# Pooled attention with a routed feed-forward: the row index moved from GpSimd to VectorE, the row fetch put one step later, and one set of transposes put behind the last values pass

## The chip, the core and the metric

The kernel runs on one core of a Trainium2 chip. The metric is the device time of one execution in microseconds (us); lower is better. Engine names below are those of the profile: PE is TensorE's matmul, PEld its weight load, DVE is VectorE, ACT is ScalarE, POOL is GpSimd, SP is SyncE, which issues most of the DMAs.

## What is computed

The reference has two blocks, one behind the other, in float32. Cut to what matters:

```python
# q, k, v: (8, 8, 1152, 64)
q_pool = q.reshape(B, H, S // 2, 2, D).mean(axis=3)
scores = np.matmul(q_pool, k.transpose(0, 1, 3, 2)) / np.sqrt(D)
scores = scores - np.max(scores, axis=-1, keepdims=True)
attn = np.exp(scores)
attn = attn / (np.sum(attn, axis=-1, keepdims=True) + 1e-09)
x = np.matmul(attn, v).transpose(0, 2, 1, 3).reshape(8, 576, 512)

# w_gate: (512,), w1: (512, 1024), w2: (1024, 512), capacity: 128
scores = np.einsum('bsd,d->bs', x, w_gate)
out = x.copy()
for b in range(B):
    top_idx = np.argpartition(-scores[b], capacity)[:capacity]
    xe = x[b, top_idx]
    h = np.maximum(xe @ w1, 0.0)
    ye = h @ w2
    g = 1.0 / (1.0 + np.exp(-scores[b, top_idx]))
    out[b, top_idx] = x[b, top_idx] + g[:, None] * ye
```

So each of the eight batches has an attention over pairs of pooled queries, then a score for each of its 576 rows; the 128 rows with the highest scores go through a two-layer feed-forward, scaled by a gate, and are added to themselves.

## The kernel before

**Halves.** The attention works on pairs of heads, four pairs for a batch, 32 pairs in all. A pair is done in two halves of 288 queries (`s` 0 and 1), so there are 64 halves, and the loop of `run` (L1322) goes over them with one more turn at the end. In each turn PE first computes the scores of half `h` (L818: 36 matmuls, 72 instructions) and then the values of half `h - 1` (L836, the same number). ACT takes the exponent of the scores in nine pieces (`p`, L825) and copies the result of the values pass out of PSUM (`two`, L844). All PSUM results go through four buffers handed out in turn by `banks`, so a matmul may have to wait until ACT has read an earlier buffer. POOL adds up parts of `p` (`acc`, L857, three instructions a half), adds the two planes of `two` (`av`, L846), multiplies with the gate's weights (`prod`, L925), normalizes (`x`, L956, in halves with `s` 1) and pools the next queries (`qp`, L732, in halves with `s` 0). DVE folds `p` and `acc` into sums (L862 twice, L872), transposes (`avb` L915, `kT` L735, `qT` L739), and computes `rec` (L954), `red`, `part` and `total` (L979, L981, L893). ACT spreads `total` into `sums` (L902) in halves with `s` 1, and copies `sum` into `groups` (L887) in halves with `s` 0.

**Units.** When the four pairs of a batch are done, `gated` starts `routed` for it, a Python generator that emits the second block in steps ("units"). Each `yield` ends a step; `units` advances every waiting generator by one step, the newest batch first. In each turn `units` is called twice: `units(mid=True)` between the scores and the values, and `units(mid=False)` at the end of the turn. A step that ended in "mid" or "hidden" goes on in the first of these, the others in the second. The order in which instructions are emitted is the order on each engine; nothing is reordered afterwards (`manual_schedule`).

For a batch below the last two, the steps are, one after the other:

- `line` (L1007, DVE) and `groups` of it (L887, ACT), then `total`, a row of scores written to DRAM and read back to all partitions (`sc_row`, `gate_sc`, SP's DMAs at L1032 to L1035);
- the gate's bound (L1069, POOL) and the comparisons that give each row its rank (`cmp` L1083 and L1092, `tie` L1102, DVE), for blocks 0 and 1 of rows, then 2 and 3 one half later, then 4 another half later, with the gate's exponent on ACT (L1115) and its sum on POOL (L1118);
- ranks and gates to DRAM and back to all partitions (`lines`, L1131 and L1135);
- one half later, the search (L1166, two instructions on DVE, the first yields the row's number, the second its gate), the index of that row in the whole output (L1175, POOL) and the fetch of the 128 rows (L1183, a DMA with an index, issued by POOL);
- a step with nothing in it, then in the middle of a turn the transposes of the fetched rows (L1197, four matmuls) and their copy `xeT` (L1200, ACT); in the middle of the next turn the first layer (L1208, 64 instructions) with its `hT` (L1216, ACT); in the middle of the next turn the second layer (L1221, 16 instructions) with `y` (L1240, ACT);
- at the end of that turn the sum (L1245, POOL) and the scatter of the rows (L1246, a DMA with an index, issued by POOL).

The batches are counted from 0. Batch 5 (`B - 3`) stops before its second layer, which is kept for the end (`waiting`), where the last batches leave PE without attention work. Batch 6 (`B - 2`) has fewer steps between, and batch 7 uses matmuls for its row of scores and its search (L1054, L1152). After the loop, `run` emits what is left of batches 5, 6 and 7 in an order written out by hand (L1397 to L1409).

The turn behind the last half (`h == n_halves`) starts with what is left of the pair before, calls `units` twice (L1362, L1363), and then emits the last values pass (`weighted`), its transposition (`drained`) and the rest.

Of the kernel before, what the change touches and what calls it, by code (L numbers as in the profile page):

```python
# [27 lines left out]
def _any_scores(  # L28
# [451 lines left out]
    in_pair = [(j, t) for j in range(2) for t in range(NF)] + [(0, NF)]  # L480
    upcoming = load_pair(*pairs[0])
    run(prepare_pair(upcoming))
    preparing = iter(())
    routing = iter(())
# [23 lines left out]
    for n, (b, hp) in enumerate(pairs):  # L508
        pair = upcoming
        run(preparing)  # L510
        if hp == 0:
            x = xpool.tile([P, NT, Dm], F32, name="x")
        for i, (j, t) in enumerate(in_pair):
            now = {"pair": pair, "j": j, "t": t, "x": x}
            advance(now)
            if two is not None and two["t"] == NF and two["pair"]["hp"] == NPAIR - 1:
                run(routing)
                routing = routed(two["pair"]["b"], two["x"])
            one, two = now, one
            if i == 0 and n + 1 < len(pairs):  # L520
                upcoming = load_pair(*pairs[n + 1])
                preparing = prepare_pair(upcoming)
            if n == 0 and i == 0:
                load_weights()
            if i >= 3:
                next(preparing, None)
            next(routing, None)
    for _ in range(2):
        advance(None)
        one, two = None, one  # L530
    run(routing)
    run(routed(B - 1, x))


class _Plain:
# [461 lines left out]
    def routed(self, b, part):  # L997


        nc, ffn, Sp, NT, NF = self.nc, self.ffn, self.Sp, self.NT, self.NF  # L1000
        tiles = [(t, P if t < NF else self.TAIL) for t in range(NT)]
        mid = "mid" if b < self.B - 2 else True
# [134 lines left out]
        for s0, w in self.slots:  # L1137
# [3 lines left out]
            if b == self.B - 1:  # L1141

                nc.vector.tensor_tensor(
                    out=pick[:, :, 0:w],
                    in0=self.slot_f[:, s0 : s0 + w].unsqueeze(1).broadcast_to([P, NT, w]),
                    in1=rank[:, :].unsqueeze(2).broadcast_to([P, NT, w]),
                    op=ALU.is_equal,
                )
                yield True
                ps = self.banks()[:, 0, 0:2]  # L1150
                for t, rows in tiles:
                    nc.tensor.matmul(  # L1152
                        ps[0:w, :],
                        lhsT=pick[0:rows, t, 0:w],
                        rhs=meta[0:rows, t, :],
                        start=(t == 0),
                        stop=(t == NT - 1),
                    )
                nc.scalar.copy(index[0:w, :], ps[0:w, 0:1])
                nc.scalar.copy(own_gate[0:w, :], ps[0:w, 1:2])  # L1160
            else:
                yield True

                found = self.small.tile([P, 1], F32, name="found_token")
                for of, to in ((self.token_line, found), (lines[:, :, 1, :], own_gate)):
                    nc.vector.scalar_tensor_tensor(  # L1166
                        out=pick.rearrange("p t i -> p (t i)").rearrange("p (i t) -> p i t", t=NT)[0:w],
                        in0=lines[0:w, :, 0, :],
                        scalar=self.token[0:w, s0 // P : s0 // P + 1],
                        in1=of[0:w, :, :],  # L1170
                        op0=ALU.is_equal,
                        op1=ALU.mult,
                        accum_out=to[0:w, :],
                    )
                nc.gpsimd.tensor_scalar(  # L1175
                    out=index[0:w, :],
                    in0=found[0:w, :],
                    scalar1=float(b * Sp),
                    scalar2=None,
                    op0=ALU.add,  # L1180
                )
            xe = ffn.tile([P, self.Dm], F32, name="xe")
            nc.gpsimd.indirect_dma_start(  # L1183
                out=xe[0:w, :],
# [122 lines left out]
    def run(self):  # L1307
        nc = self.nc
# [13 lines left out]
        for h in range(n_halves + 1):  # L1322
            if h < n_halves:
                n, s = divmod(h, 2)
                if s == 0:
                    pair = upcoming
                    if pair["hp"] == 0:
                        part = self.ffn.tile([P, self.NPAIR, self.QB], F32, name="part")
                    pair["part"] = part
                else:  # L1330
                    loaded = None
                    if n + 2 < len(pairs):
                        loaded = self.load_pair(*pairs[n + 2])
                        self.load_values(loaded)
                    if n > 1:
                        self.stored(halves[h - 4]["pair"])
                if h > 1:
                    next(weights, None)
                half = {"pair": pair, "s": s}
                halves.append(half)  # L1340
                self.scores(half)
                if h > 1:

                    of = halves[h - 2 - s]["pair"]
                    if s == 0:
                        of["groups"] = self.side_by_side(of["sum"].rearrange("p j n -> p (j n)"))
                    else:
                        self.spread(of)
                self.units(mid=True)
                if h > 2:  # L1350
                    self.gated(halves[h - 3])
                self.folded(half)
                if h > 1:
                    self.multiplied(halves[h - 2])
                if s == 0 and loaded:
                    upcoming = loaded
                    self.prepare_pair(upcoming)
            else:
                self.stored(halves[h - 3]["pair"])
                self.gated(halves[h - 3])  # L1360
                self.multiplied(halves[h - 2])
                self.units(mid=True)  # L1362
                self.units(mid=False)  # L1363
            if h > 0:
                done = halves[h - 1]
                self.weighted(done)
                self.drained(done)
            if h == n_halves:
                self.multiplied(done)
                self.gated(halves[h - 2])  # L1370
            if 1 < h < n_halves and s == 0:
                done["pair"]["total"] = self.added(done["pair"]["groups"])
            if h == n_halves:
                self.normalized(done["pair"])
            elif h > 2 and s == 1:
                self.normalized(halves[h - 2]["pair"])
            if h < n_halves:
                self.units(mid=False)
# [93 lines left out]
```

## Time and profile before

| What | Value |
|---|---|
| Median of three runs | 707.29 us (706.78 to 708.1) |
| Time of the profiled execution | 706.64 us |
| Span of the profiled execution | 704.8 us |
| Granted TensorE clock in it | 0.998 |
| PE busy | 694.4 us, 99% of the span |
| POOL busy | 485.1 us, 69% |
| DVE busy | 496.5 us, 70% |
| ACT busy | 444.5 us, 63% |
| Index (L1175), 7 instructions | 6.4 us on POOL, mean 920 ns; POOL idle before them 20.2 us |
| Fetch (L1183), 8 instructions | 9.1 us on POOL; 3.4 to 5.8 us from the instruction's start to landing, median 4.8 us |
| Scatter (L1246), 8 instructions | 8.3 us on POOL |

How to read it: the span is what the profiler saw between the first and the last instruction; the execution's own time is 1.84 us longer. A busy share says how much of the span an engine was at work, not that its work set the end. A line of the timeline has a start and a duration in us, the engine, the line of the kernel, the operation, the tiles (written<-read), the shape, a count, and in brackets the engine's idle time just before and what ended it. A line of the chain of waits has a start, a duration and what ran. Idle time of an engine other than PE costs nothing by itself here, unless PE comes to wait for it.

### The profile page before, as it was taken

The numbers are of one execution on the slowest core, as the hardware profiler recorded it, in microseconds if no ns is written. First come the engines' busy times: TensorE is split into PE (matmuls) and PEld (weight loads), VectorE is DVE, ScalarE is ACT, GpSimd is POOL, SyncE is SP. The second block draws the span as 40 slices with busy tenths as digits, with TensorE's granted clock in tenths as the row PEclk, the third lists the DMA queues.
The fourth block names the chain that finished last, engine by engine and source line by source line (L and its number), as shares of the span: only waits on it lengthen the run. The fifth ranks groups of instructions, "written<-read, shape, count | busy, mean of one in ns | idle before, by whom it ended". The sixth has DMA issues, their size and how long they took to land.

```text
span 704.8 us, 23397 instructions
## 1 busy us (share of the span) xinstructions
PE 694.4 (99%) x9948; PEld 516.8 (73%) x9948; DVE 496.5 (70%) x793; ACT 444.5 (63%) x963; POOL 485.1 (69%) x452
## 2 busy tenths in 40 slices
PE   8999999999999999999999999999999999999996
PEld 5668899996758866688656887578775787766573
DVE  3877777996559965498754988559774697689540
ACT  6677778777547775477746776467754777477210
POOL 5877777868658695586955779467874877686520
PEclk9999999999999999999999999999999999999999
DMA  8888887858486483756928468382775728432200
GB/s 175 172 178 180 171 166 137 146 116 161 85 149 111 85 162 75 145 97 111 172 40 159 81 129 160 66 148 61 161 130 85 135 56 169 83 72 62 45 31 35
DMA packets 389490, 82.86 MB, mean 118 GB/s; under 512 B 376640, under 2 KB 376640, under 8 KB 389376
## 3 DMA queue, kind: packets, MB, share of 16 engines
q1 hardware_dynamic: 387872, 76.49, 58.1%
q0 software_dynamic: 1280, 4.20, 1.8%
q8 instruction: 80, 1.31, 0.8%
q10 hardware_dynamic: 224, 0.59, 0.3%
q14 instruction: 34, 0.28, 0.1%
HBM read 69.65 MB, written 11.59 MB: 115 GB/s over the span
## 4 chain that ended last, share of the span: by engine, by line
PE 89%; POOL 5%; issue 2%; DMA 1%; ACT 1%; DVE 1%; SPq 0%; POOLq 0%; DVEq 0%; ACTq 0%
PE ps L836 36%; PE ps L818 36%; PE ps L1208 8%; PE ps L1221 7%; POOL acc L857 2%; ACT p L825 1%; DMA kb<-in_k_dram 1%; DMA xe<-out_dram,index 1%; PE ps L1197 1%; POOL prod L925 1%; POOL x L956 0%; POOL av L846 0%; DVE fold L862 0%; POOL index L1175 0%; SPq L759 0%
## 5 line engine op out<-in xcount | busy, mean ns | idle before, releaser
L825 ACT ACTIVATE p<-ps 128x576 f32<-128x576 f32 x576 | 320.2, 695 | 1.7 <-PE ps L818 1.3
L818 PE MATMUL ps<-qT,kT 64*64 64x288 f32 x4608 | 295.2, 404 | 0.2 <-ACT p L825 0.2
L836 PE MATMUL ps<-p,v_sb 64*64 64x288 f32 x4608 | 294.6, 403 | 0.0
L857 POOL TENSOR_TENSOR acc<-p 128x576 f32<-128x576 f32 x192 | 266.3, 1417 | 15.4 <-ACT p L825 15.1
L836 PEld LDWEIGHTS ps<-p,v_sb 64*64 64x64 f32 x4608 | 215.5, 133 | 65.3 <-ACT p L825 9.2
L818 PEld LDWEIGHTS ps<-qT,kT 64*64 64x64 f32 x4608 | 208.0, 132 | 73.0 <-ACT p L825 15.4
L862 DVE TRANSPOSE_TENSOR_REDUCE fold<-p 128x54 f32<-128x1728 f32 x64 | 126.0, 1969 | 50.2 <-ACT p L825 50.2
L862 DVE TRANSPOSE_TENSOR_REDUCE fold<-acc 128x54 f32<-128x1728 f32 x64 | 125.3, 1957 | 46.0 <-POOL acc L857 45.8
L844 ACT COPY two<-ps 128x576 f32<-128x576 f32 x64 | 40.9, 639 | 156.9 <-PE ps L836 143.8
L846 POOL TENSOR_TENSOR av<-two 128x288 f32<-128x288 f32 x64 | 51.2, 800 | 96.5 <-ACT two L844 94.9
L915 DVE STREAM_TRANSPOSE avb<-av 128x288 f32<-128x288 f32 x64 | 29.4, 460 | 66.5 <-POOL av L846 66.5
L956 POOL TENSOR_TENSOR x<-avb,rec 128x576 f32<-128x576 f32 x32 | 37.1, 1159 | 40.3 <-DVE rec L954 27.9
L1208 PEld LDWEIGHTS ps<-xeT,w 128*128 128x128 f32 x512 | 57.8, 192 | 2.7 <-ACT p L825 2.6
L1208 PE MATMUL ps<-xeT,w 128*128 128x128 f32 x512 | 59.3, 277 | 0.0
L1221 PE MATMUL ps<-w,hT 128*128 128x512 f32 x128 | 57.3, 598 | 0.0
L925 POOL TENSOR_TENSOR prod<-avb,w_gate 128x288 f32<-128x288 f32 x64 | 51.5, 805 | 0.6 <-DVE avb L915 0.6
L902 ACT ACTIVATE sums<-total,tiny 32x18 f32<-32x18 f32 x124 | 38.1, 308 | 15.9 <-DVE total L893 14.2
L732 POOL TENSOR_TENSOR qp<-qb 128x576 f32<-128x576 f32 x31 | 43.8, 1414 | 2.2 <-DMA qb<-in_q_dram 2.2
L1221 PEld LDWEIGHTS ps<-w,hT 128*128 128x128 f32 x128 | 23.6, 190 | 28.1 <-issue 25.8
L735 DVE STREAM_TRANSPOSE kT<-kb 128x1152 f32<-128x1152 f32 x31 | 42.5, 1370 | 0.0
L887 ACT COPY groups<-sum 32x36 f32<-32x36 f32 x124 | 27.1, 219 | 6.7 <-DVE sum L872 5.2
L981 DVE TENSOR_TENSOR part<-red,rec 128x18 f32<-128x18 f32 x32 | 27.0, 845 | 1.1
(95 smaller groups left out, 290.6 us busy)
## 6 DMA issues: line engine op xcount, KB each, us to landing
kb<-in_k_dram SPq DMA_DIRECT2D x124, 144.0 KB
qb<-in_q_dram SPq DMA_DIRECT2D x124, 144.0 KB
v_sb<-in_v_dram SPq DMA_DIRECT2D x124, 144.0 KB
out_dram<-x SPq DMA_DIRECT2D x128, 72.0 KB
lines<-row_rank SPq DMA_DIRECT2D x7, 640.0 KB
w<-in_moe_w_dram SPq DMA_DIRECT2D x8, 512.0 KB
sc_row<-row SPq DMA_DIRECT2D x7, 288.0 KB
acc<-in_q_dram ACTq DMA_DIRECT2D x2, 288.0 KB
```

The costliest lines, as they stand in the source:

```text
L732: nc.gpsimd.tensor_tensor(out=qp[:, :, :], in0=pair["q"][:, :, 0, :], in1=pair["q"][:, :, 1, :], op=ALU.add)
L735: nc.vector.transpose(kT.rearrange("p (c g i) -> p c g i", c=self.NC, i=BLK), pair["k"].rearrange("p (g c) d -> p c g d", c=self.NC),)
L818: nc.tensor.matmul(sc[keys, j, 0:n], lhsT=pair["kT"][rows, c * P + keys.start : c * P + keys.stop], rhs=pair["qT"][rows, qs], start=True, ...
L825: nc.scalar.activation(p[:, c // G, c % G, :, :], sc[:, :, 0:n], AF.Exp, scale=self.scale)
L836: nc.tensor.matmul(av[j * self.D : (j + 1) * self.D, e, 0:n], lhsT=half["pair"]["v"][keys, j, c, :], rhs=half["p"][keys, c // G, c % G, j, :],
L844: nc.scalar.copy(two[:, :, :], av[:, :, 0:n])
L846: nc.gpsimd.tensor_tensor(out=half["av"][:, :], in0=two[:, 0, :], in1=two[:, 1, :], op=ALU.add)
L857: nc.gpsimd.tensor_tensor(out=acc[:, u, :], in0=units[:, 0, u, :], in1=units[:, 1, u, :], op=ALU.add)
L862: nc.vector.tensor_reduce(fold[:, a, :], of.rearrange("p u (m d) -> p (u m) d", d=BLK), AX.X, ALU.add, apply_transpose=True,)
L925: self.nc.gpsimd.tensor_tensor(out=pair["prod"][:, ns, :], in0=pair["avb"][:, ns, :], in1=self.w_gate[:, hp : hp + 1, :].broadcast_to([P, ...
L1208: nc.tensor.matmul(pv[:, f, 0:w], lhsT=self.w1[:, c, (f0 + f) * P : (f0 + f + 1) * P], rhs=xeT[:, c, 0:w], start=(c == 0), stop=(c == self ...
L1221: nc.tensor.matmul(ps[0:w, 0 : self.Dm], lhsT=hT[:, f, 0:w], rhs=self.w2[:, f, :], start=(f == 0), stop=(f == self.NFC - 1),)
```

## The change

The index is computed by VectorE instead of GpSimd. For batches 0 to 5 a `yield True` follows it, so the fetch and everything after it is emitted one turn later than before. In the turn behind the last half, the two calls of `units` go behind the last values pass.

```diff
@@ -1172,13 +1172,16 @@
                         op1=ALU.mult,
                         accum_out=to[0:w, :],
                     )
-                nc.gpsimd.tensor_scalar(
+                nc.vector.tensor_scalar(
                     out=index[0:w, :],
                     in0=found[0:w, :],
                     scalar1=float(b * Sp),
                     scalar2=None,
                     op0=ALU.add,
                 )
+                if b < self.B - 2:
+
+                    yield True
             xe = ffn.tile([P, self.Dm], F32, name="xe")
             nc.gpsimd.indirect_dma_start(
                 out=xe[0:w, :],
@@ -1359,13 +1362,13 @@
                 self.stored(halves[h - 3]["pair"])
                 self.gated(halves[h - 3])
                 self.multiplied(halves[h - 2])
-                self.units(mid=True)
-                self.units(mid=False)
             if h > 0:
                 done = halves[h - 1]
                 self.weighted(done)
                 self.drained(done)
             if h == n_halves:
+                self.units(mid=True)
+                self.units(mid=False)
                 self.multiplied(done)
                 self.gated(halves[h - 2])
             if 1 < h < n_halves and s == 0:
```

In the order of instructions on each engine this gives the following. Lines of the kernel before are used.

- POOL, batches 0 to 5: L1175 is gone. L1183 moves from behind `av` of a half with `s` 0 to behind `x` of the next half, which has `s` 1. For batches 0 to 4, L1245 and L1246 move from behind `av` of a half with `s` 0 to behind `x` and L1069 (the next batch's) of the next half. Batch 6: L1175 is gone, L1183 stays.
- PE, batches 0 to 5: L1197 and L1208 each stand one turn later, and so does L1221 for batches 0 to 4. Batch 6: L1197 stands behind the last values pass instead of ahead of it.
- ACT, batches 0 to 5: `xeT` moves from behind `groups` of a half with `s` 0 to behind `sums` (and, for batches 0 to 4, behind the next batch's `groups` of `line`) of the next half; it stands ahead of `two` as before. `hT` and, for batches 0 to 4, `y` move by one turn too. Batch 6: `xeT` moves behind the last `two`.
- DVE: seven instructions of 128x1 more, each behind the two of the search.
- SP: its list of DMAs stays the same.

## The prediction

> **What bounds the kernel now.** I read the page's busy shares first, then the chain of waits, then the timeline of each engine around one fetch (batch 1) and around the end. PE is busy 99% of the span, so the change can only remove or add the few places where PE stands still. In the chain, a pass of 72 instructions takes 4.37 us when nothing disturbs it. Batch 4's transposes show a typical disturbance:
>
> ```profile
> PE 694.4 (99%) x9948; PEld 516.8 (73%) x9948; DVE 496.5 (70%) x793; ACT 444.5 (63%) x963; POOL 485.1 (69%) x452
> ...
> 500.73 4.38 PE ps L836 x72
> 505.11 4.61 PE ps L818 x71
> 509.72 0.59 PE ps L1197 x4
> ```
>
> The pass ahead of L1197 is 0.24 us too long. For batches 0, 1, 2 the same reading gives 0.10, 0.17 and 0.25 us. Batch 3: from L836 at 397.11 (4.39 us) five more passes should end at 423.35, and L1197 starts at 424.04: 0.69 us. Batch 5: 590.75 + 4.37 = 595.12 against 595.73: 0.61 us. Together 2.06 us. Why they wait is seen in batch 1:
>
> ```profile
> 245.51 0.92 POOL L1175 TENSOR_SCALAR index<-found_token 128x1 int32<-128x1 f32 x1 [2.96 <-DVE pick L1166]
> 246.71 1.14 POOL L1183 DMA_INDIRECT xe<-out_dram,index  x1 [0.28 <-POOL index L1175]
> 247.88 4.15 POOL L857 TENSOR_TENSOR acc<-p 128x576 f32<-128x576 f32 x3
> 239.09 0.64 ACT L844 COPY two<-ps 128x576 f32<-128x576 f32 x1 [2.48 <-PE ps L836]
> 248.16 0.64 ACT L844 COPY two<-ps 128x576 f32<-128x576 f32 x1 [2.22 <-PE ps L836]
> ```
>
> POOL stands 2.96 us for the search, and fetches late. The last L836 matmul before the two `two` lines starts at 238.59 and 247.34: `two` follows after 0.49 us normally, after 0.82 us where the fetch runs. In batches 0, 1, 2, 4, 5 it is 0.25 to 0.43 us late in this way; PE's loss is some 0.15 us less than the lateness (0.39 late, 0.25 lost in batch 2). In batches 3 and 5 the fetch itself lands too late.
>
> At the end PE waits twice more:
>
> ```profile
> 653.20 0.63 PE L1197 MATMUL ps<-ident,xe 128*128 128x128 f32 x4 [0.61 <-DMA xe<-out_dram,index]
> 664.28 1.21 PE L1054 MATMUL ps<-diag,ones 128*128 128x288 f32 x4 [0.35 <-DVE rank_parts L1076]
> ```
>
> **Part 1, the index on DVE.** POOL loses 7 x 0.92 us and the wait in front of it. DVE gets 7 instructions; the nearest row, a DVE TENSOR_SCALAR of one element (L1283), took 0.14 us, so 1 us in all. Of this only 0.15 us for each of batches 1 to 4 lies in a chain that matters (below). The index now stands behind both searches (the second takes 0.89 us), so the fetch could start at once only where POOL is free: for batch 6 it starts 0.1 us earlier.
>
> **Part 2, the fetch one turn later.** I walk through batch 1 with its own rows. POOL needn't wait for the search, so `acc` starts when `av` is done, some 3.5 us earlier. The fetch then stands behind `x`. Its start comes out at 254.65, with PE wanting the rows at 260.6: 5.9 us, against landings of 3.4 to 5.8 us. It ends at 255.8, before the next `two` is due at 256.55. So I take all 2.06 us as saved (bounds 0 and 2.06).
>
> A fetch under other DVE work is what a rule of the Trainium skill warns of (SBUF — State Buffer, "Who interferes with whom"): while VectorE runs an instruction that takes the port pair shared with GpSimd, GpSimd cannot write a DMA's descriptors. The eight fetches here took 1.06 to 1.27 us, two-microsecond folds beside them, so the rows show none of it; by the rule a fetch beside a copy of 1.37 us (L735's time) would be that much later and the sum up to 1.4 us a batch higher.
>
> **Part 3, what moves with it.** This is where I expect the loss. The sum L1245 and scatter L1246 come one turn later too, from a half in which POOL has been idle for 7 us to one where `acc` waits behind them:
>
> ```profile
> 205.60 1.28 POOL L1245 TENSOR_TENSOR xe<-y,xe 128x512 f32<-128x512 f32 x1
> 207.16 1.05 POOL L1246 DMA_INDIRECT out_dram<-xe,index  x1 [0.28 <-POOL xe L1245]
> ...
> 216.62 0.24 POOL L1069 TENSOR_SCALAR gate<-gate_sc 128x5 f32<-128x5 f32 x1
> 216.83 4.21 POOL L857 TENSOR_TENSOR acc<-p 128x576 f32<-128x576 f32 x3
> 219.62 1.97 DVE L862 TRANSPOSE_TENSOR_REDUCE fold<-p 128x54 f32<-128x1728 f32 x1
> 221.51 1.93 DVE L862 TRANSPOSE_TENSOR_REDUCE fold<-acc 128x54 f32<-128x1728 f32 x1
> ```
>
> L1069 ends some 0.45 us earlier than before (216.4, the half's fold is done sooner). Then 1.25 + 0.28 + 1.04 us: `acc` starts at 219.0 instead of 216.83 and ends at 223.2. DVE's fold of `acc`, which followed its other fold without a gap at 221.51, now waits to 223.23: 1.72 us later. From there to 239 DVE has only two gaps, 0.27 and 0.85 us, both behind POOL work (gate, `acc`) that itself follows DVE's `rec`. So the 1.72 us stays in the chain (bounds 0, if the gaps and POOL's shorter queue take it in, and 2.2). The search starts at 246.28 instead of 244.56 and ends, index included, at 248.15. The folds follow at 248.55 and 250.45 (before 252.06, having waited for POOL), `x` at 253.4 (255.02), the fetch to 255.8, `acc` at 255.83 (256.14), its fold at 260.03 (260.33), and so `total` at 264.6 (264.91). The time won on POOL is used up.
>
> Now the cover that is gone. ACT's queue in that half:
>
> ```profile
> 265.30 1.27 ACT L902 ACTIVATE sums<-total,tiny 32x18 f32<-32x18 f32 x4 [2.24 <-DVE total L893]
> 266.60 0.85 ACT L887 COPY groups<-line 32x18 f32<-32x18 f32 x4
> ...
> 273.76 0.64 ACT L844 COPY two<-ps 128x576 f32<-128x576 f32 x1 [4.01 <-PE ps L836]
> ...
> 257.22 4.54 PE L818 MATMUL ps<-qT,kT 64*64 64x288 f32 x72
> 261.70 7.41 PE L1208 MATMUL ps<-xeT,w 128*128 128x128 f32 x64
> ```
>
> `sums` waits for `total`, and `two` is behind it. This was free, since the first layer's 7.34 us of matmuls made the half long: `two` was due at 273.76. With L1208 one turn later the half holds only the transposes: scores from 256.22 to 260.59, transposes to 261.18, values (4.53 us behind them, as in the chain of before) to 265.71, `two` due 0.35 us later at 266.05. ACT's queue: `sums` 265.0 to 266.3, `groups` to 267.1, `xeT`, now here too (0.57 us), to 267.65. So `two` is 1.6 us late, the next exponents are as late, and the next scores pass finds no free buffer. By the relation above PE loses 1.6 - 0.15 = 1.45 us.
>
> Batches 1 to 4: 4 x 1.45 = 5.8 us. Batch 5 has no `groups` of `line` there (-0.85) and PE has L1021 more (0.33): 0.42 late, 0.3 lost. Batch 0 has no scatter ahead: its folds run 1.7 us earlier, `xeT` ends at 265.95 in these times, just before 266.05: 0. Sum 6.1 us. Bounds: 0, if `total` comes as early as for batch 0 in all, and 6.1 + 5 x 0.6 = 9.1, if DVE's chain is another 0.6 us later (the tie at 398.58 took 1.57 us where others took 0.62).
>
> A rule speaks for more loss: the same page and section say that a VectorE instruction with two SBUF inputs and a GpSimd instruction that reads SBUF block each other wholly. The row: `tie`, which now meets L1245, took 0.34 us alone and 0.62 to 0.92 us beside POOL's work, so it is lengthened already and I add nothing; by the rule up to 1.28 us a batch would be added to the chain.
>
> **Part 4, the end.** Before, from the values pass at 648.00 to L1054 at 664.28: 16.28 us. Now two values passes without a break (2 x 4.37), transposes 0.59, L938 0.24, L1221 5.40: 14.97. PE could be at L1054 1.31 us sooner. L1054 needs `diag`, the end of a chain over POOL and DVE that ran almost without a gap from 619 on; with batch 5's L1208 now inside the turn after, DVE has its first comparisons done before that turn ends and is some 2 us ahead there, 1.4 us ahead at batch 6's fetch. So I take 1.2 us of 1.31. Without that lead only batch 6's 0.1 us is left: bounds 0.1 and 1.31.
>
> **Sum.** -2.06 - 1.2 + 6.1 = +2.84 us. Profiled: 706.64 becomes 709.5 (span 704.8 to 707.6). The median of the runs is 0.65 us above the profiled execution: 707.29 + 2.84 = 710.1 us.
>
> **Rivals.** *A, the lead reaches PE* (faster): POOL's 3.5 us and the gaps take in the scatter, every batch goes like batch 0, nothing is lost: 707.29 - 3.26 = 704.0. For it: POOL is idle 20.2 us at the index. Against: DVE's rows without gaps. Chance 0.16. *B, a wash*: `two` comes only 0.8 us late, 4 x 0.65 = 2.6 us lost, batch 5 nothing: 707.29 - 3.26 + 2.6 = 706.6. For it: the lateness is a difference of long sums; if POOL reaches L1245 a microsecond sooner it halves. Chance 0.17. *C, worse*: the delayed `sums` of the search's own half also passes its `two`: it ends at 247.65 where `two` is due at 247.83, a margin of 0.18 us. From 0.33 us (margin plus 0.15) more delay PE pays there too; with 1 us more in batches 1 to 4, 4 x 0.67 there and as much behind it: 715.5. Chance 0.10; its near part is in the range. *D, it doesn't do what it says*: the fetch, elsewhere now, holds up `two` again, and the 2.06 us isn't saved: 712.2. Against: 0.75 us between its end and `two`. Counted in the forecast's own spread.
>
> **How the numbers follow.** Forecast 0.57 (708.7 to 713), A 0.16, B 0.17, C 0.10. A measurement of this kernel can tell 0.2%, 1.4 us, from no change, so "same" is 705.9 to 708.7. Faster 0.17 (A and a little of B), same 0.16, slower 0.67. The range is 706.0 to 713.0: below lies A, above most of C; its own bounds would be 707 to 713.
>
> **What would show it.** In the changed profile: no index on POOL and no wait there; the fetch some 5.9 us before its transposes and `two` back at 0.49 us; `acc` behind the scatter near 2 us late; then, in the half of the transposes, `sums`, `groups` and `xeT` right up to a late `two`, and a scores pass of some 5.8 us instead of 4.37 behind it, for batches 1 to 4 and not batch 0. If these passes are 4.37 us, A holds.

## The result and the profile after

The changed kernel takes 726.0 us (median of 6 runs, 725.32 to 728.61), beside 706.76 us for the kernel before (6 runs, 705.41 to 708.1): ratio 1.028, 95% interval 1.0258 to 1.0303. The prediction said slower, by 2.8 us; it is slower by 19.2 us. The profiled execution has a span of 726.0 us, 21.2 us more than before.

Line numbers behind the search are 3 higher in the changed kernel: transposes L1200, `xeT` L1203, first layer L1211, second L1224, sum L1248, scatter L1249, fetch L1186. First the busy shares of the changed kernel:

```profile
PE 703.2 (97%) x9948; PEld 497.4 (69%) x9948; DVE 507.3 (70%) x800; ACT 445.7 (61%) x963; POOL 484.9 (67%) x445
```

PE has the same 9948 instructions and a lower share: it stands still more. To find where, I take each pass of 72 matmul instructions from its start to the start of whatever PE does next, less the undisturbed 4.37 us. Added up over the passes this gives 6.5 us for the kernel before and 27.2 us for the changed one; the difference, 20.7 us, is nearly the whole 21.2. It stands in three places, which serve for all runs below: the scores pass right ahead of the transposes; the scores pass beside which the search runs ("behind the search's half"); and the scores pass of the turn behind the transposes ("behind the transposes' half"). Of the first and the last column 0.1 to 0.2 us a batch is the normal switch to another kind of matmul:

| us over the batches | ahead of the transposes | behind the search's half | behind the transposes' half | median |
|---|---|---|---|---|
| before | 3.4 | 0 | 0.7 | 706.76 |
| changed kernel | 2.5 | 6.0 | 15.8 | 726.0 |
| `index_back` | 3.3 | 6.2 | 18.1 | 730.45 |
| `scatter_gap` | 1.0 | 0 | 5.3 | 707.79 |
| `search_later` | 0.8 | 6.0 | 6.3 | 714.7 |
| `gap_search_later` | 1.0 | 0 | 0.6 | 703.62 |

Three stretches of batch 1 show how it comes about. The timeline of the changed kernel where the scatter now stands:

```profile
218.79 1.27 POOL L1248 TENSOR_TENSOR xe<-y,xe 128x512 f32<-128x512 f32 x1
220.35 1.09 POOL L1249 DMA_INDIRECT out_dram<-xe,index  x1 [0.29 <-POOL xe L1248]
...
225.65 1.98 DVE L862 TRANSPOSE_TENSOR_REDUCE fold<-acc 128x54 f32<-128x1728 f32 x1 [2.96 <-POOL acc L857]
...
231.37 1.38 DVE L1102 SCALAR_TENSOR_TENSOR tie<-sc_row,gate_sc,before 128x128 f32<-128x128 f32 x1
233.55 0.77 DVE L1102 SCALAR_TENSOR_TENSOR tie<-sc_row,gate_sc,before 128x128 f32<-128x128 f32 x1
```

DVE's fold waits 2.96 us for an `acc` that stood behind sum and scatter (before: no gap). And the next two ties take 1.38 and 0.77 us; in the kernel before the same two took 0.34 and 0.62 us. These and the two searches in the kernel before:

```profile
227.20 0.34 DVE L1102 SCALAR_TENSOR_TENSOR tie<-sc_row,gate_sc,before 128x128 f32<-128x128 f32 x1
228.34 0.62 DVE L1102 SCALAR_TENSOR_TENSOR tie<-sc_row,gate_sc,before 128x128 f32<-128x128 f32 x1
...
244.56 0.86 DVE L1166 SCALAR_TENSOR_TENSOR pick<-lines,token,token_line 128x640 f32<-128x640 f32 x1
245.46 0.89 DVE L1166 SCALAR_TENSOR_TENSOR pick<-lines,token 128x640 f32<-128x640 f32 x1
```

Then the half of the search in the changed kernel:

```profile
247.87 4.72 POOL L857 TENSOR_TENSOR acc<-p 128x576 f32<-128x576 f32 x3
249.91 1.42 DVE L1166 SCALAR_TENSOR_TENSOR pick<-lines,token,token_line 128x640 f32<-128x640 f32 x1
250.01 1.27 ACT L902 ACTIVATE sums<-total,tiny 32x18 f32<-32x18 f32 x4 [3.19 <-DVE total L893]
251.31 0.64 ACT L844 COPY two<-ps 128x576 f32<-128x576 f32 x1
251.38 1.90 DVE L1166 SCALAR_TENSOR_TENSOR pick<-lines,token 128x640 f32<-128x640 f32 x1
252.00 3.44 PE L818 MATMUL ps<-qT,kT 64*64 64x288 f32 x48 [0.60 <-ACT two L844]
252.55 1.39 POOL L925 TENSOR_TENSOR prod<-avb,w_gate 128x288 f32<-128x288 f32 x1
```

Two things at once. `total` comes so late that `sums` goes right up to `two`, and PE waits for `two`: this is the place that the prediction's rival C had named, with a margin of 0.18 us. And the two searches take 1.42 and 1.90 us instead of 0.86 and 0.89, beside an `acc` that takes 4.72 us instead of 4.14 and a `prod` that takes 1.39 instead of 0.80. Last, fetch and transposes' half:

```profile
258.44 1.16 POOL L956 TENSOR_TENSOR x<-avb,rec 128x576 f32<-128x576 f32 x1 [3.74 <-DVE rec L954]
259.75 1.13 POOL L1186 DMA_INDIRECT xe<-out_dram,index  x1 [0.16 <-issue]
...
270.06 1.27 ACT L902 ACTIVATE sums<-total,tiny 32x18 f32<-32x18 f32 x4 [4.53 <-DVE total L893]
271.35 0.85 ACT L887 COPY groups<-line 32x18 f32<-32x18 f32 x4
272.11 0.57 ACT L1203 COPY xeT<-ps 128x512 f32<-128x512 f32 x1
272.59 0.62 ACT L844 COPY two<-ps 128x576 f32<-128x576 f32 x1
272.73 3.92 PE L818 MATMUL ps<-qT,kT 64*64 64x288 f32 x56 [1.55 <-ACT xeT L1203]
```

The queue on ACT is the predicted one, `sums`, `groups`, `xeT`, `two`; what is not as predicted is how late it starts. POOL's lead of 3.5 us is gone: it waits 3.74 us for `rec`, which stands behind the searches and the folds on DVE.

### The profile page after: what moved, and what is told of

Its sections match the earlier page's. It is cut to its first block, busy times and chain, and to the rows that moved or that the text cites. A ratio compares the mean times of both kernels' runs of the same rounds, so it can differ in the third digit from the quotient of the medians.

```text
span 726.0 us, 23404 instructions
## 1 busy us (share of the span) xinstructions
PE 703.2 (97%) x9948; PEld 497.4 (69%) x9948; DVE 507.3 (70%) x800; ACT 445.7 (61%) x963; POOL 484.9 (67%) x445
## 3 DMA queue, kind: packets, MB, share of 16 engines
q8 instruction: 80, 1.31, 0.8%
## 4 chain that ended last, share of the span: by engine, by line
PE 42%; POOL 24%; issue 14%; DVE 8%; DMA 6%; ACT 5%; SPq 2%; POOLq 0%; DVEq 0%; ACTq 0%
PE ps L818 16%; PE ps L836 15%; POOL acc L857 14%; PE ps L1211 8%; DVE fold L862 3%; PE ps L1224 2%; DMA out_dram<-x 2%; POOL prod L925 2%; DVE kT L735 2%; DMA kb<-in_k_dram 2%; POOL x L956 2%; POOL av L846 2%; ACT p L825 2%; ACT sums L902 1%; POOL qp L732 1%
## 5 line engine op out<-in xcount | busy, mean ns | idle before, releaser
L818 PE MATMUL ps<-qT,kT 64*64 64x288 f32 x4608 | 302.2, 409 | 12.3 <-ACT xeT L1203 9.1
L857 POOL TENSOR_TENSOR acc<-p 128x576 f32<-128x576 f32 x192 | 269.1, 1429 | 20.4 <-ACT p L825 20.0
L818 PEld LDWEIGHTS ps<-qT,kT 64*64 64x64 f32 x4608 | 197.2, 134 | 103.9 <-ACT p L825 22.2
L836 PEld LDWEIGHTS ps<-p,v_sb 64*64 64x64 f32 x4608 | 205.6, 133 | 75.5 <-ACT p L825 10.8
L915 DVE STREAM_TRANSPOSE avb<-av 128x288 f32<-128x288 f32 x64 | 29.5, 460 | 76.6 <-POOL av L846 76.6
L1211 PEld LDWEIGHTS ps<-xeT,w 128*128 128x128 f32 x512 | 57.8, 192 | 2.7 <-ACT p L825 2.6
L1211 PE MATMUL ps<-xeT,w 128*128 128x128 f32 x512 | 59.3, 277 | 0.0
L1224 PE MATMUL ps<-w,hT 128*128 128x512 f32 x128 | 57.3, 598 | 0.0
L925 POOL TENSOR_TENSOR prod<-avb,w_gate 128x288 f32<-128x288 f32 x64 | 54.8, 856 | 0.6 <-DVE avb L915 0.6
L1224 PEld LDWEIGHTS ps<-w,hT 128*128 128x128 f32 x128 | 23.6, 190 | 28.1 <-issue 25.8
L735 DVE STREAM_TRANSPOSE kT<-kb 128x1152 f32<-128x1152 f32 x31 | 42.5, 1370 | 0.0
L1219 ACT ACTIVATE hT<-ps 128x512 f32<-128x512 f32 x16 | 9.6, 597 | 39.6 <-PE ps L1211 39.6
```

The source lines that it names most:

```text
L735: nc.vector.transpose(kT.rearrange("p (c g i) -> p c g i", c=self.NC, i=BLK), pair["k"].rearrange("p (g c) d -> p c g d", c=self.NC),)
L818: nc.tensor.matmul(sc[keys, j, 0:n], lhsT=pair["kT"][rows, c * P + keys.start : c * P + keys.stop], rhs=pair["qT"][rows, qs], start=True, ...
L836: nc.tensor.matmul(av[j * self.D : (j + 1) * self.D, e, 0:n], lhsT=half["pair"]["v"][keys, j, c, :], rhs=half["p"][keys, c // G, c % G, j, :],
L857: nc.gpsimd.tensor_tensor(out=acc[:, u, :], in0=units[:, 0, u, :], in1=units[:, 1, u, :], op=ALU.add)
L925: self.nc.gpsimd.tensor_tensor(out=pair["prod"][:, ns, :], in0=pair["avb"][:, ns, :], in1=self.w_gate[:, hp : hp + 1, :].broadcast_to([P, ...
L1211: nc.tensor.matmul(pv[:, f, 0:w], lhsT=self.w1[:, c, (f0 + f) * P : (f0 + f + 1) * P], rhs=xeT[:, c, 0:w], start=(c == 0), stop=(c == self ...
```

## The experiments

The ratios are to the kernel before, run on the same chip between them. My theory when they began had three parts: (i) the scatter stands in front of an `acc` that is waited for, (ii) `sums` waits for `total` ahead of `two` in a half made short, (iii) DVE's two-input instructions and POOL's `acc` lengthen each other at the ties and at the search.

**The index alone (`index_only`).** The first half of the diff's first hunk, in the kernel before:

```diff
-                nc.gpsimd.tensor_scalar(
+                nc.vector.tensor_scalar(
                     out=index[0:w, :],
```

> The kernel before with the index on VectorE and nothing else of the change (POOL then waits for the search in front of the fetch). My theory: the index itself costs and gives nothing, 706 to 707.5 us, searches still at 0.86 and 0.89 us because POOL still stands still beside them. Rival (the seven index instructions lengthen VectorE's chain and `sums` passes `two`): 709 us or more.

706.36 us, ratio 0.9989 (0.9979 to 0.9999): no difference that counts. The searches took 0.85 and 0.89 us. The index on DVE is harmless by itself.

**The index back on POOL (`index_back`).** The reverse edit, in the changed kernel.

> The changed kernel with the index back on POOL, so that POOL waits for the first search as it did before; the later fetch, the later steps and the moved end stay. My theory: the searches go back to 0.86 and 0.89 us (from 1.42 and 1.90), since POOL does nothing beside them, but POOL's `acc` is then as much later as VectorE is earlier, so the time stays at 724 to 729 us. Rival R1 (VectorE and POOL holding each other up at the search is what costs): the losses behind the half of the transposes shrink by about 1.6 us in each of batches 1 to 4, 717 to 720 us.

730.45 us, ratio 1.0328 (1.0308 to 1.0348). That is above the 724 to 729 us expected. The searches are at 0.86 and 0.89 us again, and the kernel is slower still: `acc` starts at 250.94, behind the index, instead of beside the search, and its fold follows at 255.12. In batch 1 it is 8.0 us from the start of the first search to the end of that fold, and 7.55 us in the changed kernel. So the long search is not a loss against waiting: not waiting gains some 0.45 us there, where POOL's `acc` starts 3.9 us earlier against the search, because the searches take 1.6 us more.

**The scatter in POOL's idle time (`scatter_gap`).** A new mark lets the step go on just ahead of the values, where POOL waits for `two`:

```diff
                 if b < self.B - 2:
-                    yield True
+                    yield "gap"
                 nc.gpsimd.tensor_tensor(out=xe[0:w, :], in0=y[0:w, :], in1=xe[0:w, :], op=ALU.add)
...
-            entry[2] = end in ("mid", "hidden") and b < self.B - 2
+            entry[2] = end if end == "gap" else end in ("mid", "hidden") and b < self.B - 2
...
+            if h < n_halves:
+                self.units(mid="gap")
             if h > 0:
                 done = halves[h - 1]
```

> The changed kernel with the sum and the scatter moved forward by half a turn, into the 8.8 us in which POOL waits for `two` in the half of the second layer, ahead of `av`; transposes and layers stay where the change put them. My theory: the fold of `acc` no longer waits 2.96 us and the ties fall from 1.38 to about 0.6 us, so VectorE's chain is some 3.3 us sooner; the 1.2 us behind the search's half are gone in batches 1 to 5 (6.0 us), and most of the 15.8 us behind the transposes' half: 706 to 711 us. Rival R2 (the cover lost in the half of the transposes is the cause, with the scatter or without): only the 6.0 us go, 718 to 721 us. Rival R1 (holding up at the search): 722 us or more.

707.79 us, ratio 1.0015 (1.0003 to 1.0027): 18.2 us of the loss are gone by moving two POOL instructions per batch by half a turn. Its timeline, batch 1:

```profile
209.74 1.26 POOL L1248 TENSOR_TENSOR xe<-y,xe 128x512 f32<-128x512 f32 x1 [4.27 <-ACT y L1243]
211.28 1.04 POOL L1249 DMA_INDIRECT out_dram<-xe,index  x1 [0.28 <-POOL xe L1248]
214.31 0.79 POOL L846 TENSOR_TENSOR av<-two 128x288 f32<-128x288 f32 x1 [1.98 <-ACT two L844]
...
221.97 1.93 DVE L862 TRANSPOSE_TENSOR_REDUCE fold<-acc 128x54 f32<-128x1728 f32 x1
...
265.31 1.27 ACT L902 ACTIVATE sums<-total,tiny 32x18 f32<-32x18 f32 x4 [2.51 <-DVE total L893]
...
267.37 0.57 ACT L1203 COPY xeT<-ps 128x512 f32<-128x512 f32 x1
267.85 0.62 ACT L844 COPY two<-ps 128x576 f32<-128x576 f32 x1
267.99 3.92 PE L818 MATMUL ps<-qT,kT 64*64 64x288 f32 x56 [0.37 <-ACT xeT L1203]
```

Sum and scatter fit between `y` and `two`, and POOL still idles 1.98 us. The fold of `acc` follows without a gap. Of the 1.55 us that PE waited for `xeT` behind the transposes' half 0.37 are left (by the table's count 1.0 of 2.2 us), with `sums` at 265.31 instead of 270.06. The searches still take 1.40 and 1.91 us here.

**The search behind the folds (`search_later`).** In the changed kernel, with the same mark and the same two additions to `units` and `run`:

```diff
                 yield True
+                if b < self.B - 2:
+                    yield "gap"

                 found = self.small.tile([P, 1], F32, name="found_token")
```

> The changed kernel with the search and the index emitted half a turn and some more later, behind the two folds of the next half, where POOL mostly stands still waiting for `rec`; all else as in the changed kernel. My theory: the searches are back near 0.9 us each, and the folds, `sum` and `rec` no longer wait for them, so POOL's `x`, the fetch and the next `acc` come 1.6 us or more sooner; the 1.2 us behind the search's half come from the scatter and stay, the loss behind the transposes' half shrinks by 1.6 us or more in batches 1 to 5: 715 to 720 us. Rival (the search's length beside POOL is hidden under POOL's own queue): 724 us or more.

714.7 us, ratio 1.0102 (1.008 to 1.0124): 11.3 us back, a little more than expected. The two searches in the list of groups of this kernel (durations are minimum, median and maximum in ns):

```profile
L1168 DVE SCALAR_TENSOR_TENSOR pick<-lines,token,token_line x7: 864/876/1033, 163.7 to 655.8; 128x640 f32<-128x640 f32 x7
L1168 DVE SCALAR_TENSOR_TENSOR pick<-lines,token x7: 885/885/887, 164.8 to 656.7; 128x640 f32<-128x640 f32 x7
```

The 6.0 us behind the search's half stay, as expected, since the scatter makes them; those behind the transposes' half fall from 15.8 to 6.3 us. Batch 0, which has no scatter ahead of it, falls from 1.23 to 0.10 us: there the search ahead of the folds is the whole loss. Note that the edit takes away two things at once, the searches' lengthening (1.6 us) and their own 1.75 us, since the folds no longer stand behind them; it does not tell the two apart.

**Both (`gap_search_later`).**

> The early scatter (scatter_gap) and the later search (search_later) together. Theory: the 1.0 us that scatter_gap still loses behind each transposes' half come from POOL's `x`, fetch and `acc` standing behind VectorE's lengthened search; with the search behind the folds these are gone too: 702 to 704.5 us, faster than the kernel before. Rival (the 1.0 us are the lost cover alone, whatever the search does): 707 to 708.5 us, as scatter_gap.

703.62 us, ratio 0.9944 (0.9927 to 0.9962), the fastest of all, 3.7 us under the kernel before. Busy shares, and ACT in the search's half of batch 1:

```profile
PE 693.6 (99%) x9948; PEld 515.9 (73%) x9948; DVE 498.7 (71%) x800; ACT 444.0 (63%) x963; POOL 478.4 (68%) x445
...
245.60 1.27 ACT L902 ACTIVATE sums<-total,tiny 32x18 f32<-32x18 f32 x4
248.78 0.64 ACT L844 COPY two<-ps 128x576 f32<-128x576 f32 x1 [1.91 <-PE ps L836]
```

`sums` ends 1.9 us before `two` is due. Note that the late fetch, the transposes' half without its cover and the end are all as in the changed kernel. The two repairs alone add up to 18.2 + 11.3 = 29.5 us, more than the 22.4 they give together: they work on the same lateness, and once `two` is in time, more lead is worth nothing.

**One more empty turn (`turn_more`).** In the changed kernel, so that transposes and layers fall on the old half of a pair:

```diff
             yield True
+            if b < self.B - 3:
+                yield True
             yield mid
```

> The changed kernel with one more empty turn behind the fetch for batches 0 to 4, so that transposes, first layer, second layer, sum and scatter fall on the same half of a pair as before the change. My theory (the loss is that the scatter stands in front of an `acc` that is waited for, and that `sums` stands ahead of `two` in a half made short): both go, the scores passes behind the search's half and behind the transposes' half are back near 4.4 us, 702 to 708 us. Rival R1 (holding up at the search): the searches still take 1.4 and 1.9 us and the time stays over 715 us.

714.8 us, ratio 1.0109 (1.0092 to 1.0126): my expectation was missed. The half that lost its first layer stays short whether the transposes are in it or not, so `sums` (267.08), `groups` and `two` (269.14) still come late there: 11.2 us. The searches still take 1.41 and 1.90 us, as rival R1 had said, and how much of the 11.2 us is theirs this run doesn't tell. And the scatter now stands ahead of the `acc` beside which the next batch's ties run:

```profile
227.04 4.13 POOL L857 TENSOR_TENSOR acc<-p 128x576 f32<-128x576 f32 x3
227.11 4.22 DVE L1102 SCALAR_TENSOR_TENSOR tie<-sc_row,gate_sc,before 128x128 f32<-128x128 f32 x1
```

A tie that took 0.62 us before takes 4.22 us: it ends when the three `acc` do, and these keep their 4.13 us. So it goes in each of batches 1 to 5 (4.21 to 4.22 us).

**`sums` behind `two` on ACT (`sums_behind`).** In the changed kernel:

```diff
-                    else:
-                        self.spread(of)
...
+            if 1 < h < n_halves and s == 1:
+                self.spread(of)
             if 1 < h < n_halves and s == 0:
```

> The changed kernel with one thing moved on ACT: in halves with s 1, `sums` is emitted behind `two` instead of ahead of it. The sum, the scatter, the search and the transposes stay where the change put them, so VectorE's chain is as late as in the changed kernel. My theory: PE loses its time only because `two` stands behind a `sums` that waits for `total`; the scores passes behind the search's half (6.0 us) and nearly all behind the transposes' half (15.8 us) are back near 4.4 us: 704 to 711 us. Rival (VectorE's and POOL's lateness reaches PE by another way, through `kT`, the exponents or `x`): 718 us or more.

742.26 us, ratio 1.0491 (1.0468 to 1.0514). As a way to mend the kernel it failed, and the size was far off my expectation:

```profile
263.25 0.64 ACT L844 COPY two<-ps 128x576 f32<-128x576 f32 x1 [3.21 <-PE ps L836]
263.92 1.27 ACT L902 ACTIVATE sums<-total,tiny 32x18 f32<-32x18 f32 x4
265.21 5.00 ACT L825 ACTIVATE p<-ps 128x576 f32<-128x576 f32 x9
265.91 2.89 PE L818 MATMUL ps<-qT,kT 64*64 64x288 f32 x40 [0.81 <-ACT p L825]
```

ACT's free time lies ahead of `two` (3.21 us here); behind it the exponents follow at once, and PE needs their buffers. So 1.27 us put there cost 1.2 to 1.6 us in 30 halves, 39 us in all, in halves that the change never touched too. Behind the transposes' halves of batches 1 to 4 the loss is now 1.4 us each instead of 2.2 to 4.2, just the price of an uncovered `sums`. But this doesn't tell my theory from its rival: with every pair 1.3 us longer DVE had time to catch up, and in batch 1 `total` ended at 281.1, 1.7 us ahead of `two`. For that question the run is inconclusive.

**The end alone (`tail_only`).** Only the diff's second hunk, in the kernel before.

> The kernel before with only the two calls of `units` moved behind the last values pass. Theory (the prediction's term for the end): 1.2 us less, 705.2 to 706.3 us beside 707.2 for the kernel before. Rival (the chain to `diag` sets the end, so that only 0.1 us is gained without the lead that the prediction counted on): 706.8 to 707.5 us.

707.55 us, ratio 1.0001 (0.9988 to 1.0014): nothing; the rival was right. The same chain to `diag` sets the end, and PE's wait only moved to L1054, where it was 0.35 us before:

```profile
665.75 1.21 PE L1054 MATMUL ps<-diag,ones 128*128 128x288 f32 x4 [1.29 <-DVE rank_parts L1076]
```

**The late scatter alone (`scatter_alone`).** In the kernel before, one more turn ahead of the sum:

```diff
                 if b < self.B - 2:
                     yield True
+                if b < self.B - 3:
+                    yield True
```

> The kernel before with only the sum and the scatter one turn later (batches 0 to 4), where the change puts them; fetch, search, transposes and layers as before. Theory: `acc` behind the scatter is about 2 us late, the ties of the next blocks meet POOL's `acc` and are longer, and the 1.2 us behind the search's half appear in batches 1 to 5 (6 us), while the transposes' half keeps its cover of first-layer matmuls and loses nothing: 711 to 715 us. Rival (the late scatter costs only together with the lost cover): 706.5 to 708.5 us.

723.38 us, ratio 1.0229 (1.0191 to 1.0267): more than expected. The timeline of batch 1 tells why:

```profile
223.44 1.98 DVE L862 TRANSPOSE_TENSOR_REDUCE fold<-acc 128x54 f32<-128x1728 f32 x1 [2.97 <-POOL acc L857]
...
248.71 0.92 POOL L1175 TENSOR_SCALAR index<-found_token 128x1 int32<-128x1 f32 x1 [2.99 <-DVE pick L1166]
249.90 1.13 POOL L1183 DMA_INDIRECT xe<-out_dram,index  x1 [0.28 <-POOL index L1175]
...
255.90 0.63 PE L1197 MATMUL ps<-ident,xe 128*128 128x128 f32 x4 [2.61 <-DMA xe<-out_dram,index]
```

The fold starts 1.93 us later than before (221.51), and the index 3.20 us later (245.51): of the difference, 1.27 us, 1.20 are the ties' (1.39 and 0.77 us instead of 0.34 and 0.62). With the fetch in its old place, PE then also waits 2.61 us for the fetched rows, which I had not counted; over the run these waits are 10.6 us, and about 6 us are left for the late `two`, as expected. The changed kernel has no such wait: its later fetch hides it, and this is a point in its favour.

**The lost cover alone (`cover_alone`), and both (`scatter_cover`).** In the kernel before, the layers one turn later; in the first with the scatter in POOL's idle time as above, in the second without:

```diff
             nc.scalar.copy(xeT[:, :, 0:w], pv[:, 0 : self.ND, 0:w])
             yield mid
+            if b < self.B - 2:
+                yield mid
```

> The kernel before with first and second layer one turn later (batches 0 to 5), so that the half in which the first layer stood has no extra matmuls, and the sum and scatter in POOL's waiting time ahead of `av` (as in scatter_gap), so that they delay nothing; fetch, search and transposes as before. Theory: from the rows of before `total` at 264.9 us ends `sums` and `groups` at 267.4, where `two` would be due at 265.5: 1.9 us late, 1.7 us lost in each of batches 0 to 4 and about 0.9 less in batch 5: 713 to 717 us. Rival (without a late scatter or a lengthened search `sums` still comes in time): 706.5 to 709 us.

> The kernel before with both of the preceding: first layer, second layer, sum and scatter one turn later, where the change puts them; fetch, index and transposes as before, and the end as before. Theory: both delays add up on the same `sums`, 6 us behind the search's half and 3 to 4 us behind the half without its matmuls in each batch: 726 to 733 us, so the later steps by themselves cost as much as the whole change or more, and the index and the later fetch give a little back. Rival (the fetch and the lengthened search are a large part of the loss): 712 to 720 us.

709.46 us, ratio 1.0035 (1.0011 to 1.0059), and 727.37 us, ratio 1.0293 (1.0276 to 1.031). The first is less than I expected: the passes lose 1.1 us, not 1.7, in batches 1 to 4 (5.9 us in all), and 1.8 us are won back ahead of the transposes. The second is as expected in size, but not in place. Only 3.0 us are lost where the moved layers take the cover away; 18.6 us are lost ahead of the transposes. Some 6 of these are the late `two` of the search's half, as in the changed kernel, but 11.3 are five waits for the fetched rows, one of them here:

```profile
256.37 0.63 PE L1197 MATMUL ps<-ident,xe 128*128 128x128 f32 x4 [1.89 <-DMA xe<-out_dram,index]
```

The changed kernel, with its later fetch, waits for no rows and loses 15.8 us behind the transposes' half instead. So it is chance that the two times are nearly the same: the run does not show that the moved layers and scatter account for the loss of the whole change.

**One input (`one_input`).** In the changed kernel, the second search:

```diff
-                for of, to in ((self.token_line, found), (lines[:, :, 1, :], own_gate)):
+                for of, to in ((self.token_line, found),):
...
+                nc.vector.tensor_scalar(
...
+                    in0=lines[0:w, :, 0, :],
+                    scalar1=self.token[0:w, s0 // P : s0 // P + 1],
+                    scalar2=None,
+                    op0=ALU.is_equal,
+                    op1=ALU.add,
+                    accum_out=own_gate[0:w, :],
+                )
```

> The changed kernel with the second search replaced by a comparison with one SBUF input of the same 128x640 elements (it counts the matches; the gate is not fetched, so the output's gate is another). It tells whether it is the two SBUF inputs that make the search long beside POOL's `acc`, as the Trainium skill states (SBUF — State Buffer, "Who interferes with whom"). If so: it takes 0.8 to 0.95 us in batches 0 to 5, about 1 us less than the 1.90 us of the second search, the first search stays at 1.42 us, and the kernel's time falls to 720 to 723 us. Rival (any VectorE instruction is held up there): 1.6 us or more, 725 to 727 us.

719.56 us, ratio 1.0169 (1.015 to 1.0188), 6.4 us under the changed kernel. The two instructions (L1166 has two inputs, L1175 is the new one), POOL beside them in batch 1, and one of the first kind, in batch 2:

```profile
L1166 DVE SCALAR_TENSOR_TENSOR pick<-lines,token,token_line x7: 861/1415/4292, 158.9 to 663.8; 128x640 f32<-128x640 f32 x7
L1175 DVE TENSOR_SCALAR_CACHE_REDUCE pick<-lines,token x7: 878/879/880, 160.4 to 664.7; 128x640 f32<-128x640 f32 x7
...
245.56 4.72 POOL L857 TENSOR_TENSOR acc<-p 128x576 f32<-128x576 f32 x3
250.24 0.79 POOL L925 TENSOR_TENSOR prod<-avb,w_gate 128x288 f32<-128x288 f32 x1
...
336.11 4.29 DVE L1166 SCALAR_TENSOR_TENSOR pick<-lines,token,token_line 128x640 f32<-128x640 f32 x1
338.93 0.79 POOL L846 TENSOR_TENSOR av<-two 128x288 f32<-128x288 f32 x1
```

With one input all seven take 0.88 us, whatever POOL does. With two inputs the median is 1.42 us, and one took 4.29 us, till 0.7 us after POOL's `av` ended (the profiled execution, 722.86 us, is the longest of the four). And each search lengthened its own neighbour: in batch 1 `acc`, beside the first search, still takes 4.72 us, while `prod` is back from 1.39 to 0.79 us. In batch 0 the loss behind the transposes' half falls from 1.23 to 0.22 us, by the 1.0 us that the second search is shorter.

The new instruction is another operation too, not only one with one input. The traces of before and after help here. `part` (L981), a TENSOR_TENSOR with two inputs, took 0.18 us in the changed kernel in the five cases where POOL only issued the scatter beside it, and 0.62 to 0.92 us in the 27 others, beside POOL's work, mostly `acc` and `x`; the one-input comparisons of L1092 took 0.40 us (128x192) and 0.27 us (64x64) beside POOL's work, and the same the one time each when POOL did nothing. So two different operations with two inputs are lengthened, and those with one are not.

## Why the prediction was right or wrong

The direction and the mechanism of the prediction's part 3 were right: `sums`, `groups` and `xeT` right up to a late `two`, behind a scatter that delays `acc`. The size was not: a loss of 6.1 us was forecast where some 21 us came. By its own steps:

- **Index on DVE, 0.14 us each, no effect:** right (0.14 us; `index_only` within 0.2%).
- **The stalls ahead of the transposes, 2.06 us, all saved:** half right. In the changed kernel they fell by 0.9 us only; what PE still waits for there is `p` on ACT (1.5 us in three batches), not the fetch. With scatter and search repaired they fell by 2.3 us. The descriptor rule that was weighed there (the Trainium skill, SBUF — State Buffer, "Who interferes with whom") doesn't show: the eight fetches of the changed kernel took 1.05 to 1.27 us, as those before. But it was not put to the test: DVE ran sums and folds beside them and no copy, and L735, whose 1.37 us the prediction took for a copy's, is a transposition.
- **The scatter delays DVE's chain by 1.72 us (bounds 0 and 2.2):** this step failed. In `scatter_alone` it is 1.93 us at the fold and 3.20 us at the index. What was left out is the ties: the prediction let `tie` meet only L1245, judged it "lengthened already" and added nothing, but the late `acc` shifts onto the ties of blocks 2 and 3, and two of them take 1.2 us more. (The prediction read 0.34 us as a tie's time alone; a tie can have it beside `acc` too, as in the kernel before at 227.20, with `acc` from 224.58 to 228.82.) The rule that it had weighed and set aside (same page and section: a VectorE instruction with two SBUF inputs and a GpSimd instruction that reads SBUF block each other) gave up to 1.28 us a batch, and this case's rows (1.2 us at the ties, 1.6 us at the searches) are nearer to it than to nothing.
- **POOL starts `acc` 3.5 us earlier, beside the search, and the search keeps its 0.86 and 0.89 us:** this step failed too, and for the same reason. Two-input searches beside `acc` and `prod` took 1.42 and 1.90 us, 1.6 us more in DVE's chain. `one_input` takes 1.0 us of it away and wins 6.4 us; `search_later` takes the whole search out from ahead of the folds and wins 11.3. The fetch, forecast for 1.6 us ahead of its half's scores pass (254.65 and 256.22), started with that pass (259.75 and 259.69).
- **The search's half loses nothing (margin 0.18 us, rival C at 0.10):** wrong; 1.2 us in each of batches 1 to 5, 6.0 us. With 3.2 us of delay instead of 1.72 the margin was crossed in all five.
- **The transposes' half loses 1.45 us in batches 1 to 4, 0.3 in batch 5, none in batch 0 (6.1 us):** right place, mis-sized: 15.8 us, with 2.2 to 4.2 us in batches 1 to 4, 1.65 in batch 5 and 1.23 in batch 0. The lost cover with no late scatter and no lengthened search costs 5.9 us (`cover_alone`, where `xeT` doesn't stand ahead of `two`); with the search behind the folds it costs nothing (`gap_search_later`). So I put the rest down to the two steps above, which arrive at the same `sums`.
- **The end, -1.2 us of 1.31:** right. In the changed kernel the stretch from the values to L1054 is 685.36 - 670.31 = 15.05 us, 1.23 less than before, and L1054 doesn't wait:

```profile
670.31 8.96 PE L836 MATMUL ps<-p,v_sb 64*64 64x288 f32 x144
679.20 0.66 PE L1200 MATMUL ps<-ident,xe 128*128 128x128 f32 x4
...
685.36 1.21 PE L1054 MATMUL ps<-diag,ones 128*128 128x288 f32 x4
```

`tail_only` shows the condition that the prediction had named: without the other parts of the change DVE has no lead there, and the gain is nil. That the lead comes from batch 5's moved first layer was not tried by itself.

Rival A's sum (every batch without loss, 704.0 us) is what `gap_search_later` reached, 703.62 us, with the scatter and the search moved: the gains were counted well (2.3 and 1.23 us there, 2.06 and 1.2 forecast). The loss came of the place of the scatter and of what POOL and DVE do beside each other. What stays open: how the 15.8 us split between scatter, search and cover, since the parts don't add up; and why one two-input instruction beside `acc` keeps its 0.34 us, another is held up by 0.5 us and a third until POOL is done.

## What to carry to other kernels

When a wait is taken from one engine, ask what it will run in that time beside the other engines, and if both read SBUF and one of them is a two-input VectorE instruction, take that they run one after the other as the upper bound (in batch 1 here the overlap gained 0.45 us). When a chain of steps moves by one turn, look for each step's new neighbour in the queue, the last one of the chain (here the scatter) first, and put it where its engine already waits. An engine's idle time counts only where it lies in its own order: ACT's was ahead of `two`, and 1.27 us put behind it cost 1.2 to 1.6 us each time.

## What the runs showed of the hardware

- A VectorE instruction with two SBUF inputs and POOL's sums lengthen each other, from 0.86 to 1.42 us and 0.89 to 1.90 us for a search, up to 4.22 us for a tie of 0.62 us and 4.29 us for a search of 0.86 us; POOL's three `acc` went from 4.14 to 4.72 us and `prod` from 0.80 to 1.39 us beside the searches, but stayed at 4.13 us beside the tie of 4.22 us (`turn_more`).
- The same elements through a one-input comparison took 0.88 us all seven times, in batches 0 to 5 beside the same work on POOL (`one_input`).
- A VectorE TENSOR_TENSOR of 128x18 with two inputs took 0.18 us beside POOL's scatter and 0.62 to 0.92 us beside its work on `acc`, `x` and the like (`after`).
